# Linear attention, gated GLU and SoLU in one kernel: the first phase in nine equal blocks of 512 tokens

## The chip, the cores and the metric

The kernel runs on one core of one Trainium2 chip. The metric is the device time of one execution in microseconds; most executions of one kernel agree within 0.3%. The engines are TensorE (PE), VectorE (DVE), ScalarE (ACT), GpSimd (POOL) and SyncE (SP), which here only issues DMAs.

## The reference, cut to what matters

Inputs are double precision (the 64-bit weights are turned into pairs of single-precision parts on the chip, below). For 8 batches of 576 tokens, 8 heads of 64:

```python
q_s = exp(q - max(q, -1)); q_s /= sum(q_s, -1) + 1e-9        # softmax over the head dimension
k_s = exp(k - max(k, 2));  k_s /= sum(k_s, 2) + 1e-9         # softmax over the tokens of a batch
x = einsum('bhsd,bhde->bhse', q_s, einsum('bhsd,bhse->bhde', k_s, v))
x = x.transpose(0, 2, 1, 3).reshape(4608, 512)
g = x @ w_gate                                               # 512 x 1536
y = (g * sigmoid(g) * (x @ w_val)) @ w_out                   # 1536 x 512
h = y @ w_in                                                 # second layer, 512 x 1024
s = h * softmax(h)
out = ((s - mean(s)) / sqrt(var(s) + 1e-6) * g_ln) @ w_out2  # 4608 x 512
```

A block of tokens needs all k and v of its batch before its first product with x (the k softmax runs over the tokens), but only its own rows of q.

## The kernel before, in words

**Phase 1** makes y for all 4608 tokens and stores it; **phase 2** reads it back and does the second layer in 36 tiles of 128 tokens. Phase 2 is not touched except for where its tiles lie.

Products are made in single precision parts: every operand is a high part (rounded to the matmul's format) and a low part (the rest), and `mm3` does three matmuls for one product: high x high, high x low, low x high.

**Blocks and steps.** Phase 1 goes block by block over tokens. In a block, the 1536 inner columns are twelve steps `f` of 128. A step is 12 matmuls of the gate product (`emit_g`, then ScalarE's silu, L850), 12 of the output product of an earlier step (`next_o`, L805 to L807 into `y`), and 12 of the value product (`emit_v`, then `v_rest`: VectorE multiplies, `st`, L855; ScalarE rounds, `ah`, L859; VectorE subtracts, `al`, L861). The output product of step f comes two steps later. Gate and value products and all small products share four PSUM banks. The blocks before: two of 288 tokens (batch 0), seven of 512, one of 448.

**Weights.** Eighteen 1 MB pieces: twelve `wgv` (gate and value of one step) and six `wo` (output of two steps). Each comes as 64-bit words and is converted on the chip by `Weight.convert`, in five steps that a `Task` can take one by one: ScalarE scales the high words (L231), the low words are shifted down to three bits (L234 on ScalarE or L238 on VectorE, chosen by `l3`: before, two of three pieces on ScalarE), ScalarE writes the rounded high word over the upper half of the low word (L242), VectorE joins them (L245), rounds to the high part (L258) and subtracts for the low part (L260). Thirteen pieces fit in SBUF; eight `wgv` are stored after conversion and streamed in again for every later block through three slots (`STREAM`, `TURNS`). The pieces of the second layer's weights are converted one a block (`conv_w2`).

**The startup before.** A `Clock` puts the work of the startup in order by nominal times written in `KEYS`: tasks are taken by due time, one generator step at a time, and this fixes the order of each compute engine's instructions. The prologue makes batch 0's k-v products and x; the clock's stream `products` then runs the two 288-token blocks in two chunks of six steps (`fch`), block 0 and block 1 in turn, so that each converted weight serves both blocks before the next is wanted. Chunk one leaves a partial y of both blocks in DRAM (`y_part`), which `y_fix` adds in blocks 3 to 6. The conversions lie between the products by their times in `conv`; k, v and q of batch 1 and of the third block are loaded and worked off at the times `e0`, `e1`, `e2`, late in the startup.

**The blocks after the startup.** From the third block on, order is written out: `block` merges the steps (gate at position 3n, output at 3n+1, value at 3n+2) with a dictionary of extra tasks at such positions (`tasks_of`): k's maximum and exponential and k-v products of the next batch, q of the next block, its transposition by DMA (`q_turn`), its parts (`q_split`), its x (`x_mm`), weight streaming. Under `manual_schedule` each engine, SP included, runs its instructions in just this order.

Of the kernel before, what the change touches and what calls it, by code (L numbers as in the profile page):

```python
# [19 lines left out]
P = 128  # L20
# [7 lines left out]
    ld=(0, 1, 2, 5, 3, 6, 4, 8, 7),  # L28
# [10 lines left out]
    go=27.8,  # L39
    conv=(17.35, 22.1, 27.85, 28.0, 30.65, 34.25, 35.8, 40.3, 45.7, 50.5, 54.15, 58.15, 62.6, 68.25, 72.6, 77.45, 82.05, 87.15),  # L40
    q1=(23.5, 26.45, 29.5, 30.9, 32.2, 1.0),
    e0=(93.3, 94.1, 100.3, 102.55, 102.4),
    e1=(97.1, 107.55, 112.6, 116.3, 118.8),
    e2=(100.5, 110.4, 116.1, 120.3, 125.5, 1.5),
    warm=((3.5, 18), (10.25, 1), (15.02, 1), (18.81, 8), (19.15, 5), (19.65, 2), (22.83, 7), (25.42, 3), (29.44, 7), (30.61, 2), (34.75, 1)),
    store=(48.0, 50.0, 52.0, 54.0, 56.0, 90.0, 92.0, 94.0),
    banks=3,
    fch=(6,),
    l3=(3, 2),
    hi=(1, 0),  # L50
    d={'km': 1.3, 'kb': 0.5, 'rs': 1.3, 'kvh': 0.3, 'kvl': 0.3, 'qh': 0.4, 'ql': 0.4, 'xh': 0.4, 'xl': 0.5, 'w1': 1.1, 'w2': 1.0, 'w3': 1.0, 'w4': 1.3, 'w5': 1.1, 'mm': 0.37, 'ev': 1.0, 'ah': 0.6, 'al': 0.9, 'qn': 1.0},
    late=27.81,
# [65 lines left out]
def attention_glu_solu_kernel(  # L118
# [38 lines left out]
    QC = T // SP  # L157
# [34 lines left out]
    FCH = [range(a, b) for a, b in zip((0, *KEYS['fch']), (*KEYS['fch'], NF))]  # L192
# [4 lines left out]
    y_part = dram.tile([2, len(FCH) - 1, KD, P, T], F32, name="y_part")  # L197

# [5 lines left out]
    class Weight:  # L204
# [21 lines left out]
        def convert(self, pool, tag, bufs):  # L226
# [26 lines left out]
            if self.scales is None:  # L253
                hi, lo = (y.rearrange("p a m -> p (a m)") for y in (hi, lo))
                if (self.no or 0) % KEYS['hi'][0] < KEYS['hi'][1]:
                    nc.scalar.copy(out=hi, in_=x)
                else:
                    nc.vector.tensor_copy(out=hi, in_=x)  # L258
# [30 lines left out]
    def conv():  # L289

        n = len(conv_tasks)
        if n >= 2:
            conv_tasks[n - 2].finish()
        need(early_t or len([x for x in x_done if x[0] == 0]) == NPAIR)
        args = (att0, "t", 2) if early_t else (att, ("vt", "qt")[n % 2], 1)
# [22 lines left out]
    def weight(key):  # L318
        w, a = W[key]
        if w.no is not None:  # L320
            need(w.no < len(conv_tasks))
            conv_tasks[w.no].finish()
        return w.hi[:, a], w.lo[:, a]
# [7 lines left out]
    def stream_store(f):  # L331
        w, _ = W["wg", f]
        need(w.no < len(conv_tasks))
        conv_tasks[w.no].finish()
        w.store(w1_dram[streamed.index(f)])
# [30 lines left out]
    def stream_next(j, e):  # L366
# [5 lines left out]
        if STREAM[e] is None:  # L372
            load_w2(j - 2)
        else:
            stream_load(STREAM[e])
# [32 lines left out]
    def v_load(pool, b, h0):  # L408
        for t in conv_tasks:
            t.finish()  # L410
        need(b == 0 or len(conv_tasks) >= len(conv_todo))
# [156 lines left out]
    def q_load(pool, j, raw_pool=None, tag="qt"):  # L568
        b, half = divmod(j, 2)
        if j >= 2:  # L570
            x = pool.tile([BLOCKS[j][1] // 4, 4, H, D], F32, tag=tag, bufs=1, name=tag)
            for b, s, ps in segments(j):
                rows = q[b, :, s:s + 4 * (ps.stop - ps.start), :].rearrange(
                    "h (p c) d -> p c h d", c=4
                )
                for c in range(4):
                    nc.sync.dma_start(out=x[ps, c], in_=rows[:, c])
            qt_t[j] = x, x
            return
        qt_t[j] = heads_load(  # L580
            pool, tag, 1, q[b, :, half * T:(half + 1) * T, :], H, QC, raw_pool
        )
# [8 lines left out]
    def q_max(pool, j, hs):  # L591
        q_step(j, hs, 1)
        need(j != 1 or {(0, 0), (0, 1)} <= kv_done)
# [5 lines left out]
        nc.gpsimd.tensor_tensor(  # L599
# [8 lines left out]
    def q_norm(pool, j, hs):  # L608
# [7 lines left out]
        nc.gpsimd.tensor_tensor(  # L616
# [6 lines left out]
    def q_transpose(ps, pool, j, pr):  # L623
        qt = qt_t[j][1]
        need(q_at[j, 2 * pr] == 3 and len(qT_t) < 2)
        pq = ps.tile([P, QC, SP], F32, tag="gv", name="pq")
        for c in range(QC):
            nc.tensor.transpose(
                out=pq[:, c, :], in_=qt[:, c, 2 * pr:2 * pr + 2, :].rearrange("p h d -> p (h d)"), identity=ident[:SP, :SP]
            )  # L630
        qh = pool.tile([P, T], F32R, tag="qh", bufs=qb, name="qh")
        ql = pool.tile([P, T], F32R, tag="ql", bufs=qb, name="ql")
        qhv = qh.rearrange("e (p c) -> e c p", c=QC)
        qlv = ql.rearrange("e (p c) -> e c p", c=QC)
        yield d["qh"]
        nc.scalar.copy(out=qhv, in_=pq)
        yield d["ql"]
        nc.vector.tensor_tensor(out=qlv, in0=pq, in1=f32(qhv), op=ALU.subtract)
# [9 lines left out]
    def q_turn(pool, j):  # L648

        n = BLOCKS[j][1] // 4  # L650
        (wp, wt), tt = ((pool, "kt"), "vt") if j == 2 else ((tmp, "yt"), "qt")
        w = wp.tile([n, 2, 4 * H * D], U16, tag=wt, bufs=1, name="qw")
# [3 lines left out]
        qw_t[j] = wT = pool.tile([P, 2, 4, NPAIR, n], U16, tag=tt, bufs=1, name="qwT")  # L656
# [26 lines left out]
    def x_mm(ps, j, pr):  # L683
# [41 lines left out]
    def tasks_of(j):  # L725
# [7 lines left out]
        if j < B:  # L733
            for n, (load, rows, sub, exp, mm) in enumerate(((0, 2, 5, 9, 11), (12, 17, 20, 24, 26))):
                h0 = n * HG
                if n:
                    at(t, load, kv_load, att, j, h0)
                    at(t, load, v_load, att, j, h0)
                at(t, rows, kv_max_rows, att, j, h0)
                at(t, sub, kv_max_all, att, j, h0)  # L740
                at(t, exp, kv_exp, j, h0)
                for u in range(2):
                    at(t, mm, kv_mm, ps_at, att, j, h0, u)
        at(t, 15, conv_w2, j - 2, 3)
        at(t, 23, conv_w2, j - 2)
# [14 lines left out]
        at(t, 24, store_w2, j - 2)  # L760
        at(t, 25, stream_next, j, STREAM.index(None))
        if 3 <= j < 7:
            y_fix(t, (j - 3) // 2, 2 * ((j - 3) % 2))
        return t

    def kv_next(j):

        if j < B:
            kv_load(att, j, 0)
            v_load(att, j, 0)  # L770
# [8 lines left out]

    def y_fix(t, j, d):  # L780

        tiles = []

        def load(n, src):
            if not tiles:
                y = tmp.tile([P, 2, 2, T], F32, tag="yt", bufs=1, name="fix")
                tiles.extend((y[:, 0], y[:, 1]))
            nc.sync.dma_start(out=tiles[n], in_=src[d:d + 2].rearrange("k p t -> p k t"))

        def add():  # L790
            nc.vector.tensor_tensor(out=tiles[0], in0=tiles[0], in1=tiles[1], op=ALU.add)

        def store():
# [551 lines left out]
```

## Time and profile before

| | us |
|---|---|
| median of three runs | 1427.79 (1425.69 to 1430.31) |
| the profiled execution | 1428.78 |
| its span | 1426.9 |
| PE busy in the span | 1384.3 |
| DVE busy | 728.1 |
| ACT busy | 695.2 |
| POOL busy | 143.8 |
| first gate product starts | 36.30 |
| first gate product of the third block starts | 200.87 |

The span is the time between the first and the last instruction of the profiled execution. Busy times count an engine's own instructions. PE's is drawn out by overlapping matmuls, so a PE that is busy all the time may still be slower at a lower granted clock. A row of a view gives start, duration, engine, line of the kernel, operation, what it writes and reads, and in brackets how long the engine had been idle and what ended the wait.

### The profile page before, as it was taken

The page shows a single profiled execution, that of the slowest core. Times are in us where ns is not written, and L with a number is a line of the kernel's source. Part 1 is how long each engine was busy: PE and PEld are TensorE (multiplying, and loading weights), DVE is VectorE, ACT ScalarE, POOL GpSimd, SP SyncE. Part 2 cuts the span into 40 slices and gives each one's busy share as a digit, 9 for nine tenths or more (in the row PEclk, how much of TensorE's full clock was granted, in tenths as well). Part 3 has the DMA queues.
Part 4 walks back from the last instruction along what each step waited for, and adds up shares of the span by engine and source line. Part 5 has one row for each costly group of instructions (what it writes and reads, how often), then busy time and mean ns, then how long its engine had stood idle before and what let it go on. Part 6 is the DMA issues. An engine that isn't in the chain of part 4 may idle for free.

```text
span 1426.9 us, 18380 instructions
## 1 busy us (share of the span) xinstructions
PE 1384.3 (97%) x7263; PEld 1174.8 (82%) x7263; DVE 728.1 (51%) x1220; ACT 695.2 (49%) x927; POOL 143.8 (10%) x112
## 2 busy tenths in 40 slices
PE   7797899999999999999999999999999999999998
PEld 6797788888888888888888888899888888888887
DVE  6767744544544544434434422422257666666663
ACT  6986445425425425425525514331246665566563
POOL 3000302103103102102102002000000000000000
PEclk9899899999999999999999999999999999999999
DMA  9956285556566665675565263473334444544441
GB/s 257 344 168 183 62 208 171 122 164 189 136 170 171 149 181 146 152 194 139 143 179 143 99 193 92 148 265 118 144 73 104 104 97 78 106 97 101 103 78 37
DMA packets 255621, 207.11 MB, mean 145 GB/s; under 512 B 208048, under 2 KB 228528, under 8 KB 243760
## 3 DMA queue, kind: packets, MB, share of 16 engines
q1 hardware_dynamic: 255536, 205.95, 53.8%
q8 instruction: 57, 0.93, 0.3%
q14 instruction: 28, 0.23, 0.1%
HBM read 142.87 MB, written 38.01 MB: 127 GB/s over the span
## 4 chain that ended last, share of the span: by engine, by line
PE 85%; ACT 7%; DVE 5%; DMA 1%; issue 1%; POOL 0%; SPq 0%; ACTq 0%; DVEq 0%; POOLq 0%
PE wg L805 6%; PE y L806 6%; PE y L807 6%; PE y L805 6%; PE wv L805 6%; PE wv L807 6%; PE wv L806 6%; PE wg L807 6%; PE wg L806 6%; PE y L1236 4%; PE y L1235 4%; PE y L1234 4%; PE ph L1123 4%; PE ph L1125 4%; PE ph L1124 4%; PE pk L532 1%
## 5 line engine op out<-in xcount | busy, mean ns | idle before, releaser
L855 DVE TENSOR_TENSOR st<-st,wv 128x512 f32<-128x512 f32 (+2 forms) x120 | 75.9, 632 | 346.6 <-PE wv L807 320.4
L859 ACT CAST ah<-st 128x512 fp32r<-128x512 f32 (+2 forms) x120 | 70.5, 587 | 369.4 <-DVE st L855 369.3
L806 PE MATMUL y<-al,wo 128*128 128x512 f32 (+2 forms) x480 | 179.2, 373 | 8.5 <-DVE al L861 8.5
L805 PE MATMUL y<-ah,wo 128*128 128x512 f32 (+2 forms) x480 | 179.0, 373 | 8.7 <-ACT ah L859 5.3
L805 PE MATMUL wg<-xh,wgv 128*128 128x512 f32 (+2 forms) x480 | 180.2, 375 | 3.2 <-DVE wgv L258 3.2
L807 PE MATMUL wg<-xh,wgv 128*128 128x512 f32 (+2 forms) x480 | 178.2, 371 | 0.7 <-DVE wgv L260 0.7
L805 PE MATMUL wv<-xh,wgv 128*128 128x512 f32 (+2 forms) x480 | 178.5, 372 | 0.0
L807 PE MATMUL y<-ah,wo 128*128 128x512 f32 (+2 forms) x480 | 178.3, 372 | 0.0
L806 PE MATMUL wv<-xl,wgv 128*128 128x512 f32 (+2 forms) x480 | 178.1, 371 | 0.0
L807 PE MATMUL wv<-xh,wgv 128*128 128x512 f32 (+2 forms) x480 | 178.0, 371 | 0.0
L806 PE MATMUL wg<-xl,wgv 128*128 128x512 f32 (+2 forms) x480 | 178.0, 371 | 0.0
L861 DVE TENSOR_TENSOR al<-st,ah 128x512 fp32r<-128x512 f32 (+2 forms) x120 | 85.3, 711 | 68.5 <-ACT ah L859 68.4
L1236 PE MATMUL y<-w,zl 128*128 128x512 f32 (+1 forms) x296 | 113.7, 384 | 0.7 <-DVE zl L1205 0.7
L1234 PE MATMUL y<-w,zh 128*128 128x512 f32 (+1 forms) x296 | 113.6, 384 | 0.0
L1235 PE MATMUL y<-w,zh 128*128 128x512 f32 (+1 forms) x296 | 113.5, 383 | 0.0
L1123 PE MATMUL ph<-w,yh 128*128 128x512 f32 x288 | 112.9, 392 | 0.0
L1125 PE MATMUL ph<-w,yl 128*128 128x512 f32 x288 | 112.8, 392 | 0.0
L1124 PE MATMUL ph<-w,yh 128*128 128x512 f32 x288 | 112.6, 391 | 0.0
L806 PEld LDWEIGHTS y<-al,wo 128*128 128x128 f32 x480 | 91.9, 191 | 23.5 <-DVE al L861 9.8
L805 PEld LDWEIGHTS y<-ah,wo 128*128 128x128 f32 x480 | 91.6, 191 | 23.9 <-ACT ah L859 5.7
L850 ACT ACTIVATE st<-wg 128x512 f32<-128x512 f32 (+2 forms) x120 | 67.1, 559 | 88.7 <-PE wg L807 88.4
L805 PEld LDWEIGHTS wg<-xh,wgv 128*128 128x128 f32 x480 | 91.2, 190 | 17.4 <-DVE wgv L258 3.4
(239 smaller groups left out, 2424.2 us busy)
## 6 DMA issues: line engine op xcount, KB each, us to landing
wgv<-w_dram SPq DMA_DIRECT2D x64, 1024.0 KB, 5.3
vt<-in_v_dram SPq DMA_DIRECT2D x64, 144.0 KB, 4.7
yr<-y_dram SPq DMA_DIRECT2D x9, 1024.0 KB, 5.9
w_dram<-wgv SPq DMA_DIRECT2D x8, 1024.0 KB, 9.3
w_dram<-w2r SPq DMA_DIRECT2D x8, 1024.0 KB, 3.9
w<-w_dram SPq DMA_DIRECT2D x8, 1024.0 KB, 4.9
kt<-in_k_dram SPq DMA_DIRECT2D x56, 144.0 KB, 5.3
out_dram<-ot SPq DMA_DIRECT2D x58, 128.0 KB, 2.4
```

The costliest lines, as they stand in the source:

```text
L805: nc.tensor.matmul(out=po, lhsT=wh, rhs=rh, start=start, stop=False)
L806: nc.tensor.matmul(out=po, lhsT=wh, rhs=rl, start=False, stop=False)
L807: nc.tensor.matmul(out=po, lhsT=wl, rhs=rh, start=False, stop=stop)
L855: nc.vector.tensor_tensor(out=st, in0=st, in1=pv, op=ALU.mult)
L859: nc.scalar.copy(out=ah, in_=st)
L861: nc.vector.tensor_tensor(out=al, in0=st, in1=f32(ah), op=ALU.subtract)
L1123: nc.tensor.matmul(out=po, lhsT=yh[:, kk, s], rhs=wh, start=(kk == 0), stop=False)
L1124: nc.tensor.matmul(out=po, lhsT=yh[:, kk, s], rhs=wl, start=False, stop=False)
L1125: nc.tensor.matmul(out=po, lhsT=yl[:, kk, s], rhs=wh, start=False, stop=(kk == KD - 1))
L1234: nc.tensor.matmul(out=po[:, s], lhsT=zh[:, c, :], rhs=wh[:, s], start=first, stop=False)
L1235: nc.tensor.matmul(out=po[:, s], lhsT=zh[:, c, :], rhs=wl[:, s], start=False, stop=False)
L1236: nc.tensor.matmul(out=po[:, s], lhsT=zl[:, c, :], rhs=wh[:, s], start=False, stop=last)
```

## The change

Phase 1 goes in nine blocks of 512 tokens. The two 288-token blocks, their chunks, `y_part` and `y_fix` are gone. The prologue now loads 512 rows of q at once (128 partitions in place of 96) and transposes them on PE in four pieces a pair of heads; it ends with three converted weights and x of the first block. It runs to its end before the first product.

The first block then runs as the later ones do, by positions written out, with `first_tasks` in place of `tasks_of`. Fifteen conversions lie in its first ten steps, one in even steps and two in odd ones: the first three operations (L231, L234 or L238, L242) right behind the gate product of step n, the rest (L245, L258, L260) behind the value product of the same step, for weights that are used two steps later. `l3` now sends the shift of two of three pieces to VectorE. The temporary of the conversion has one buffer. Batch 1's k and v and the next q are loaded between the middle weights, worked off in the first block, and its large elementwise subtractions and products go to VectorE instead of GpSimd. k's maximum over a partition's six tokens is made by five elementwise maxima in every block. Later blocks keep their positions, with the batch worked off in block j now j + 1. Line numbers in the rows and in the text are those of the kernel before.

```diff
 KEYS = dict(
-    ld=(0, 1, 2, 5, 3, 6, 4, 8, 7),
+    ld=(0, 1, 2, 5, 3, 6, 4, 7),
...
-    conv=(17.35, 22.1, 27.85, 28.0, 30.65, 34.25, 35.8, 40.3, 45.7, 50.5, 54.15, 58.15, 62.6, 68.25, 72.6, 77.45, 82.05, 87.15),
...
+    conv=(17.35, 22.1, 27.85),
...
-    l3=(3, 2),
+    l3=(3, 1),
...
-    BLOCKS = [(0, T), (T, T)]
-    while BLOCKS[-1][0] + BLOCKS[-1][1] < NT:
-        c0 = sum(BLOCKS[-1])
-        BLOCKS.append((c0, min(TM, NT - c0)))
+    BLOCKS = [(c0, TM) for c0 in range(0, NT, TM)]
...
+    def conv_start(n):
+
+        need(n == len(conv_tasks) and not early_t)
+        conv_tasks.append(Task(conv_todo[n].convert, (tmp, "t2", 1)))
+        for _ in range(3):
+            conv_tasks[n].step()
+
+    def conv_end(n):
+
+        need(all(t.done for t in conv_tasks[:n]))
+        conv_tasks[n].finish()
...
-        nc.vector.tensor_reduce(
-            out=m, in_=raw.rearrange("p c h d -> p h d c"), axis=AX.X, op=ALU.max
-        )
+        for c in range(1, KC):
+            nc.vector.tensor_tensor(
+                out=m, in0=m if c > 1 else raw[:, 0], in1=raw[:, c], op=ALU.max
+            )
...
-    def q_max(pool, j, hs):
+    def q_max(pool, j, hs, eng=nc.gpsimd):
...
-        nc.gpsimd.tensor_tensor(
+        eng.tensor_tensor(
             out=qt, in0=raw, in1=qm.to_broadcast([n, nc_, nh, D]), op=ALU.subtract
         )
...
     man.enter_context(tc.manual_schedule())
-    for j in range(2, NB - 1):
+    for n, x in enumerate(mid):
+        if n == 3:
+            kv_next(0)
+        if n == 5:
+            q_next(0)
+        load_w1(w_b, f"b{n}", *x)
+    nc.sync.dma_start(out=g_sb, in_=g_ln.rearrange("(c p) -> p c", p=P))
+
+    def first_tasks():
...
+        t = {}
+        n_conv = len(conv_tasks)
+        again_tags = iter(("a0", "a1", "a3", "a4", "b0"))
+        for n in range(NF - 2):
+            for _ in range(1 + n % 2):
+                at(t, 3 * n, conv_start, n_conv)
+                at(t, 3 * n + 2, conv_end, n_conv)
+                nm, i = order[n_conv]
+                if nm == "wgv" and i in streamed:
+                    at(t, 3 * n + 3, stream_store, i)
+                n_conv += 1
+        need(n_conv == len(order))
+        for f in range(2):
+            at(t, 0, stream_store, f)
+        for n, x in enumerate(again):
+            tag = next(again_tags)
+            at(t, 3 * n + 2, load_w1, w_b if tag == "b0" else wpool, tag, *x)
+        at(t, 2, kv_max_rows, att, 1, 0)
+        at(t, 8, kv_max_all, att, 1, 0, HG)
+        at(t, 12, kv_exp, 1, 0)
+        at(t, 14, q_max, att, 1, ALLH, nc.vector)
+        at(t, 14, kv_mm, ps_at, att, 1, 0, 0)
+        at(t, 14, kv_mm, ps_at, att, 1, 0, 1)
+        at(t, 15, kv_load, att, 1, HG)
+        at(t, 15, v_load, att, 1, HG)
+        at(t, 18, q_exp, 1, ALLH)
+        at(t, 20, q_norm, att, 1, ALLH, nc.vector)
+        at(t, 24, q_turn, att, 1)
+        at(t, 26, kv_max_rows, att, 1, HG)
+        at(t, 26, kv_max_all, att, 1, HG, HG)
+        at(t, 29, x_tiles, ph1x, 1)
+        at(t, 30, kv_exp, 1, HG)
+        at(t, 32, kv_mm, ps_at, att, 1, HG, 0)
+        at(t, 32, kv_mm, ps_at, att, 1, HG, 1)
+        for p in range(NPAIR):
+            at(t, 29 + p, q_split, att, 1, p)
+            at(t, 31 + p, x_mm, ps_at, 1, p)
+        at(t, 33, kv_next, 1)
+        at(t, 34, q_next, 1)
...
+    block(0, range(NF), y_of(0), first_tasks())
+    for j in range(1, NB - 1):
         block(j, range(NF), y_of(j), tasks_of(j))
```

## Rows read from the trace of the kernel before

**Rows 1.** Busy time by stretch: length, busy by engine (instructions), granted clock, DMA share, GB/s
```profile
36.30:134.00 97.70, 83.33 (x568) 79.84 (x567) 70.92 (x99) 83.41 (x86) 3.34 (x2) 0.93 0.69 234
200.87:1026.00 825.13, 825.13 (x4235) 694.51 (x4234) 341.34 (x576) 326.56 (x440) 94.41 (x37) 1.00 0.56 159
```
**Rows 2.** The chain that ended last, in order of time: start, length, what
```profile
179.92 7.37 DMA qwT<-qw
```
**Rows 3.** Timeline: two steps of a 512-token block on VectorE; 448-token matmuls on PE
```profile
304.23 0.69 DVE L855 TENSOR_TENSOR st<-st,wv 128x512 f32<-128x512 f32 x1 [6.51 <-PE wv L807]
...
312.39 0.69 DVE L855 TENSOR_TENSOR st<-st,wv 128x512 f32<-128x512 f32 x1 [6.09 <-PE wv L807]
...
949.68 0.36 PE L806 MATMUL wv<-xl,wgv 128*128 128x448 f32 x1
...
951.30 0.37 PE L805 MATMUL wg<-xh,wgv 128*128 128x448 f32 x1
```
**Rows 4.** Timeline of VectorE at the end of the prologue
```profile
37.70 0.46 DVE L702 TENSOR_TENSOR xl<-y,xh 128x288 fp32r<-128x288 f32 x1
38.08 0.70 DVE L238 TENSOR_SCALAR wo0r<-wo0r 128x1024 uint32<-128x1024 uint32 x1
```
**Rows 5.** Timeline of ScalarE and VectorE in the startup: waits of one conversion
```profile
129.27 2.58 ACT L242 CAST wo5r<-wo5r 128x1024 f16<-128x1024 f32 x1 [2.62 <-DVE wo5r L238]
...
131.89 1.23 DVE L245 SCALAR_TENSOR_TENSOR t<-wo5r 128x1024 uint32<-128x1024 uint32 x1 [2.35 <-ACT wo5r L242]
```
**Rows 6.** Timeline: a conversion's pieces on ScalarE and VectorE
```profile
244.69 1.11 ACT L231 ACTIVATE w2r0r<-w2r0r 128x1024 f32<-128x1024 f32 x1
...
58.36 2.60 ACT L242 CAST wo1r<-wo1r 128x1024 f16<-128x1024 f32 x1
60.60 1.32 ACT L234 ACTIVATE wgv4r<-wgv4r,floor_bias 128x1024 uint32<-128x1024 uint8 x1
...
267.40 0.69 DVE L861 TENSOR_TENSOR al<-st,ah 128x512 fp32r<-128x512 f32 x1 [0.69 <-ACT ah L859]
268.01 1.22 DVE L245 SCALAR_TENSOR_TENSOR t<-w2r0r 128x1024 uint32<-128x1024 uint32 x1
269.26 0.69 DVE L258 CAST w2r<-t 128x1024 fp32r<-128x1024 f32 x1
269.99 1.23 DVE L260 TENSOR_TENSOR w2r<-t,w2r 128x1024 fp32r<-128x1024 f32 x1
```
**Rows 7.** VectorE by group from 200 us on; then timelines of k's and q's operations
```profile
L598 DVE TENSOR_REDUCE qm<-qt 128x32 f32<-128x2048 f32 x6 | 13.7, 2280 | 0.0
...
217.27 0.43 DVE L441 TRANSPOSE_TENSOR_REDUCE r<-m 96x8 f32<-96x256 f32 x1
...
219.39 0.44 DVE L457 STREAM_TRANSPOSE mt<-mb 96x256 f32<-96x256 f32 x1
...
233.58 0.15 DVE L542 TENSOR_SCALAR rs<-pk 128x1 f32<-128x1 f32 x1
...
235.30 0.16 DVE L542 TENSOR_SCALAR rs<-pk 128x1 f32<-128x1 f32 x1
...
145.61 1.28 ACT L523 ACT_TABLE_LOAD   x1
146.91 1.48 ACT L523 ACTIVATE kt<-kt 96x1536 f32<-96x1536 f32 x1
```
**Rows 8.** Timeline of VectorE: first split and last x part of a PE-bound block
```profile
279.61 0.46 DVE L666 COPY z<-qwT 128x512 uint16<-128x512 uint16 x1
...
297.04 0.68 DVE L702 TENSOR_TENSOR xl<-px,xh 128x512 fp32r<-128x512 f32 x1
```
**Rows 9.** Timeline of PE behind a gap in the startup
```profile
167.94 0.61 PE L806 MATMUL y<-al,wo 128*128 128x288 f32 x1 [2.53 <-DVE al L861]
...
172.66 0.44 PE L807 MATMUL wv<-xh,wgv 128*128 128x288 f32 x1
...
173.22 0.29 PE L807 MATMUL wv<-xh,wgv 128*128 128x288 f32 x1
```

More of the change, by code (lines that the diff above doesn't have):

```diff
@@ L254, in convert @@
                 hi, lo = (y.rearrange("p a m -> p (a m)") for y in (hi, lo))
[L255 to L258, printed above, removed]
+                nc.vector.tensor_copy(out=hi, in_=x)
                 yield d["w5"]
@@ L291, in conv @@
         n = len(conv_tasks)
[L292 to L295, printed above, removed]
+        args = (att0, "t", 2) if early_t else (tmp, "t2", 1)
+        if n >= args[2]:
+            conv_tasks[n - args[2]].finish()
         task = Task(conv_todo[n].convert, args)
@@ L566, in segments, with q_load @@
             done += m
[L568 to L578, printed above, removed]
-            return
-        qt_t[j] = heads_load(
-            pool, tag, 1, q[b, :, half * T:(half + 1) * T, :], H, QC, raw_pool
-        )
+    def q_load(pool, j, raw_pool=None):
+        n = BLOCKS[j][1] // 4
+        if raw_pool is not None:
+            raw = raw_pool.tile([n, H, 4, D], F32, tag="raw8", bufs=1, name="raw")
+            nc.sync.dma_start(
+                out=raw.rearrange("p h c d -> p h (c d)"),
+                in_=q[0, :, 0:4 * n, :].rearrange("h (p c) d -> p h (c d)", c=4),
+            )
+            qt_t[j] = raw.rearrange("p h c d -> p c h d"), lambda: pool.tile(
+                [n, 4, H, D], F32, tag="qt", bufs=1, name="qt"
+            )
+            return
+        x = pool.tile([n, 4, H, D], F32, tag="qt", bufs=1, name="qt")
+        for b, s, ps in segments(j):
+            rows = q[b, :, s:s + 4 * (ps.stop - ps.start), :].rearrange(
+                "h (p c) d -> p c h d", c=4
+            )
+            for c in range(4):
+                nc.sync.dma_start(out=x[ps, c], in_=rows[:, c])
+        qt_t[j] = x, x
     q_at = {}
@@ L778, in y_of @@
         return y_dram[:, :, BLOCKS[j][0]:sum(BLOCKS[j])]
[L780 to L793, printed above, removed]
-            nc.sync.dma_start(out=y_of(j)[d:d + 2].rearrange("k p t -> p k t"), in_=tiles[0])
-        need(len(FCH) == 2)
-        at(t, 6, load, 0, y_of(j))
-        at(t, 6, load, 1, y_part[j, 0])
-        at(t, 11, add)
-        at(t, 12, store)
     acts = {}
@@ L994, in attention_glu_solu_kernel @@
-    e = K["e2"]
-    clock.at(K["e0"][0], q_load, att, 2)
-    clock.at(e[0], q_max, att, 2, ALLH)
-    clock.at(e[1], q_exp, 2, ALLH)
-    clock.at(e[2], q_norm, att, 2, ALLH)
-    clock.at(e[3] - .01, x_tiles, ph1x, 2)
-    clock.at(e[3], q_turn, att, 2)
-    for p in range(NPAIR):
-        clock.at(e[4] + e[5] * p, q_split, att, 2, p)
-        clock.at(e[4] + e[5] * p + 2.0, lambda p=p: x_mm(ps_at, 2, p))
     for n, x in list(enumerate(early))[n_a:]:
         load_w1(wpool, f"a{n}", *x)
+    with tc.manual_schedule(engines=COMPUTE):
+        clock.run()
@@ L1008, in attention_glu_solu_kernel @@
+    early_t.clear()
+    pro.close()
+    pro_ps.close()
     wb = ExitStack()
     psA = ExitStack()
-    def late_loads():
-        for t in conv_tasks:
-            t.finish()
-        need(len(k_done) == NPAIR and not callable(qt_t[1][1]))
-        early_t.clear()
-        pro.close()
-        w_b = wb.enter_context(tc.tile_pool(name="wb", bufs=1, reuse_waits="tile"))
-        nc.sync.dma_start(out=g_sb, in_=g_ln.rearrange("(c p) -> p c", p=P))
-        for n, x in enumerate(mid):
-            load_w1(w_b, f"b{n}", *x)
-        w_bs.append(w_b)
@@ new lines, in attention_glu_solu_kernel @@
+    nc.sync.dma_start(out=g_sb, in_=g_ln.rearrange("(c p) -> p c", p=P))
[39 more added lines that the diff above has]
+        at(t, 34, q_next, 1)
+        for e, f in enumerate(STREAM):
+            if f is not None and e > STREAM.index(None):
+                at(t, 3 * f + 2, stream_next, 0, e)
+        return t
```

187 lines of the change are left out of this document (50 added, 137 removed).

## The prediction

> **What bounds the kernel now.** I read the busy times by stretch first. From the start of the third block (200.87 us) to the end of phase 1 (1026), TensorE is busy all the time at full granted clock, and VectorE and ScalarE are busy about 40% of it [rows 1]. So there only PE's own work counts. In the startup, from the first gate product at 36.30 us to 134, PE is busy 83.33 of 97.70 us at a granted clock of 0.93, ScalarE for as long, VectorE 70.92 us [rows 1]. The chain of waits says the same: up to 134 us it runs through the weight conversions, then through the second batch's k, v and q, as far as the transposing DMA of 7.37 us [rows 2]. All that the change can win or lose lies before the moment when the first block runs at PE's own pace. I call the start of the first gate product T0 (now 36.3) and the start of the first product of the block after the startup B (now 200.87).
>
> **What is fixed behind B.** One step of a 512-token block (gate, output, value product, 36 matmuls) takes 312.39 - 304.23 = 8.16 us, 0.2267 us a matmul; at 448 tokens it is (951.30 - 949.68) / 8 = 0.2025 us [rows 3]. Behind B the kernel now takes 1426.9 - 200.87 = 1226.0 us. After the change the blocks behind B are eight of 512 in place of seven of 512 and one of 448: 432 x 0.0242 = 10.5 us more. At B two output products are still owed; they grow from 288 columns (0.128 us a matmul, in proportion) to 512: 24 x 0.099 = 2.4 us. The last x products and one more batch border add about 0.6. So the new span is B + 1226.0 + 13.5 = B + 1239.5, and the change breaks even at B = 187.4. The two additions on VectorE for the partial y, and the DMAs around them, go; PE hides them today, so they are worth nothing. The output rows need fewer stores, at most 0.3 us at the very end.
>
> **If PE set the pace in the first block**, it would take 12 x 8.16 = 97.9, plus some 6 us, taken by columns, for the k-v products and the next x: 104 us. With T0 = 37.7 this is B = 142, a span of 1381. So the question is what the fifteen conversions do to the two engines that work beside PE.
>
> **T0.** The prologue keeps its order. Its last link is ScalarE's cast of weight 1, then VectorE, then the last x; the last x part starts at 37.70 [rows 4]. The second q block leaves VectorE, which saves one reduction, less than 2.3 us by its size; x, q and their products grow from 288 to 512 columns, 0.1 to 0.25 us an instruction on some eight instructions of the chain. The loads carry the same bytes up to here, with more q ahead of v. I take T0 = 37.7, with 36 to 41 as bounds.
>
> **The order that the change writes down.** Each engine runs its instructions in the order of the program; an instruction that waits holds all behind it. In the changed first block, step n issues on ScalarE: silu(n), then for each conversion of the step the 2^-112 scaling (L231) and the cast to the sign half (L242), then ah(n). On VectorE: the low-word shift (L238; for two of three conversions, none of these on ScalarE), st(n), al(n), and then the second half (L245, L258, L260) of each conversion of this step. Even steps have one conversion, with its shift on ScalarE; odd steps have two, both with the shift on VectorE. L242 needs the shift. The wait exists today: L242 of wo5 sits 2.62 us for VectorE's shift, and then VectorE sits 2.35 us for L242 [rows 5]. What is new is that both sit in each other's order in every pair step: the shift stands behind the former step's conversions, ah(n) stands behind both L242, al(n) behind ah(n), the second halves behind al(n).
>
> One cycle of a pair step and a single step, from X, when the shift lets L242 start. ScalarE: L242 occupies it 2.24 (58.36 to 60.60), L231 1.11, L242 2.24, so ah starts at X + 5.6. VectorE meanwhile has only a shift and st to do. al starts some 0.66 behind ah (behind st's 0.69 it waits 0.69 for ah, so st to al is 1.38), and the next instruction 0.61 behind al: X + 6.9. Second halves of 3.12 each (268.01, 269.26, 269.99, 1.23 less a start overlap): two of them end at X + 13.1. Then st(n+1), 1.38 to al, 0.61, one more second half 3.12, a shift of 0.70 [rows 3, 4, 6]: X + 18.9, where the next pair starts. ScalarE's own single conversion (some 4.6) lies inside. PE needs 16.3 for the two steps and waits. So each cycle costs 18.9 plus whatever else stands on VectorE between a single's second half and the next shift, and the change puts just there:
> - step 2: the k maximum across rows, 2.56 (217.27 to 219.83), and its subtraction, now on VectorE, 96x1536: 1.8 (between 1.7 and three times the 0.69 of 512 columns): 4.4.
> - step 4: q's maximum 2.28 and its subtraction, same size, 2.3 (at most four times 0.69, 2.8); then two k-v tails of 1.72 each, VectorE and ScalarE by turns: 8.0. Behind them ScalarE reloads the silu table, does silu and L231 before it can start L242: 1.6 more. 9.6.
> - step 6: q's sum, reciprocal and product 5.1, and the exponential with its table load on ScalarE, which delays ah by 0.6: 5.7.
> - step 8: the q copy 1.1, k's maximum in five instructions of 96x256 at 0.44, 2.2 (today one reduction), maximum across rows and subtraction 4.4: 7.7.
> Together 27.4 [rows 3, 7]. On the way these operations were hidden today where they run in PE-bound blocks; here their cover is gone.
>
> Start: the conversion of wo0 now ends behind the last x. L242 for it starts at T0 + 2.6, its second half ends at 8.4, then st(0), ah(0) behind conversion 2's first half at 11.2, al, second half to 15.6, k's maximum 2.2, shift: X of the first pair = T0 + 18.5. The first weight of step 2 is there at about T0 + 15.6, while PE would want it at 10.9.
>
> End: the last pair's second halves end at X + 13.1. Behind them stand the four q splits and x casts, which take 297.04 + 0.68 - 279.61 = 18.1 us in a PE-bound block [rows 8], here with an exponential (1.48 and a table load, 1.28) and two k-v tails (3.4) in the same order; less some overlap, 23.5.
>
> Sum: B = 37.7 + 18.5 + 4 x 18.9 + 27.4 + 13.1 + 23.5 = 195.8. Span 195.8 + 1239.5 = 1435.3. The profiled execution took 1428.78 for a span of 1426.9, so 1.9 more: 1437.2. It lies 1.0 above the median of the runs shown (1427.79), so I predict 1436, 0.6% slower.
>
> The table loads: here a load is 1.28 us and the next instruction starts 0.02 behind it [rows 7]. The Trainium skill (ScalarE: Activation LUTs, "What ACT_TABLE_LOAD costs") counts a drain of about 1.38 us on top, 2.66 a switch. That is not what this trace shows; by the page the three switches on the path would add some 4 us, an estimate that I leave out.
>
> **Loads and queues.** SP now issues k and v of batch 1 behind three of the seven middle weights and the next q behind five, and must pass each in order. The seven weights are 7.3 MB, k, v and q 2.2 MB; at the 234 GB/s of this stretch [rows 1] all 9.6 MB are there 41 us after T0, while the last of the weights is wanted at about 75. The k of batch 1 is wanted 15.6 behind T0 and has four loads' time, some 16 us: it may cost a few us, or nothing. I take nothing. The stores of converted weights and the reloads into their slots wait in SP's queue for PE and VectorE, but each has two or more steps until it is used. POOL has only two fills in this block and nothing queues behind them.
>
> **Rivals.**
> 1. Full overlap (other side). The order costs nothing, because waits are short and each engine catches up; then the busiest engine's sum ends the block. VectorE's is 12 x 1.38 + 16 x 3.12 + 10 x 0.7 + about 35 for k, q and x = 108.5; B = 146, time 1387. For it: each of the three sums is within 108. Against: rows 5, both directions. Decides if pair steps start 8 to 9 us apart. 0.08.
> 2. Half overlap: the extra VectorE work falls into its 5 us of idle time per pair, so the 27.4 mostly vanish; about 1411. It would need an order other than the one written. 0.12.
> 3. Near even, 1424 to 1432: as forecast, with cycles 1 to 2 us shorter or a shorter end. 0.17.
> 4. Slower still: PE's clock. After a gap of 2.53 us at 167.94, matmuls of 288 columns last 0.44 us in place of 0.29 until 172.9, the lower of the two levels, 1.2 in place of 2.4 GHz [rows 9]. At half rate for 5 us, each such gap costs PE 2.5 us, as much as its slack of 18.9 - 16.3 in a cycle without extra work. If PE then ends the steps, the ten gaps of the block add up to some 12 us on top: 1448. 0.15.
> The rule of the Trainium skill for rival 4 (TensorE: Matmul & The Clock Gate, "What's actually happening") is that "the default state is throttled, and activity releases the throttle"; these rows agree.
>
> **Chances.** Forecast 0.48, its own range 1427 to 1447 (T0 -1.7 to +3, cycles +-1 each, the end +-4). With the rivals: 0.2 faster by over 0.3% (below 1423.5; 0.3% is about what can be told from no change), 0.17 within, 0.63 slower. For eight in ten I take 1412 to 1451.
>
> **What would show it.** Right: in the first block, VectorE's L245 waits for ah or L242 in each odd step, L242 waits for L238, pair steps lie 23 to 28 us apart, wgv products wait for L258 or L260, granted clock below 0.95, B near 196, behind it no idle PE. Wrong: B under 187; pair steps 16 to 17 us apart; long waits for DMA in the block; PE idle behind B.

## The result and the profile after

The changed kernel takes 1439.58 us, the median of four runs (1438.16 to 1440.36), where the kernel before took 1427.65 in the same series (1425.69 to 1430.31). The ratio is 1.0081, with a 95% interval of 1.0063 to 1.0100: slower by 0.8%. 1436.0 was predicted, with 1412 to 1451. The profiled execution of after took 1439.01 us for a span of 1436.8. One execution of ten in experiment 3 took 2610.55 us where the other nine took 1424 to 1426; all times are medians. Line numbers from here on are those of the changed kernel.

Busy time by stretch of after, the answer to [rows 1]; columns: length, busy of PE, PEld, DVE, ACT and POOL (instructions), granted clock, DMA share, GB/s.

```profile
46.00:198.70 152.70, 111.47 (x511) 88.53 (x511) 103.03 (x145) 95.67 (x88) 0.28 (x2) 0.82 0.60 167
198.70:1028.00 829.30, 829.30 (x4197) 688.76 (x4196) 329.90 (x618) 328.84 (x439) 94.37 (x37) 1.00 0.54 153
```

The first block ends at B = 198.64 (before, the point that answers to it is 200.87, but by then 576 tokens are done there, here 512). In the block no engine is busy all the time: PE 73%, VectorE 67%, ScalarE 63% of 152.70 us. The block lasts 1.37 times as long as the busiest engine works in it; when all have slack, a chain that runs from one to the other sets the time. The waits of the same stretch say between which two (engine, waiting operation, what it waits for: us in all, times, the longest):

```profile
DVE al L819 <- ACT ah L818: 33.9, 11, 7.0
...
PE px L684 <- ACT qh L663: 16.3, 1, 16.3
ACT kvh L535 <- DVE rs L531: 12.1, 4, 8.8
...
PE pk L520 <- ACT kt L511: 10.2, 1, 10.2
ACT wgv11r L226 <- DVE wgv11r L222: 9.5, 1, 9.5
...
ACT wgv5r L226 <- DVE wgv5r L222: 7.3, 1, 7.3
ACT wgv9r L226 <- DVE wgv9r L222: 6.7, 1, 6.7
```

VectorE waits for ScalarE's ah, ScalarE's cast (L226, before L242) waits for VectorE's shift (L222, before L238), by turns: both directions of [rows 5], now in each other's order. After the st at 47.48 us and until 196, neither of the two waits once for PE, and in the whole stretch none of the three waits for a DMA. So PE follows: the first gate product of step 2 starts 0.15 us behind the cast of its weight (L239, before L258).

```profile
54.21 0.69 DVE L239 CAST wgv<-t 128x1024 fp32r<-128x1024 f32 x1
...
55.05 0.47 PE L771 MATMUL wg<-xh,wgv 128*128 128x512 f32 x1 [2.23 <-DVE wgv L239]
```

The gate products at 68.28, 121.27 and 146.35 start 0.15 us behind their cast too, though the view puts these waits down to a shift on ScalarE that had ended long before. ScalarE's timeline at the casts that open the five pair steps:

```profile
59.01 2.58 ACT L226 CAST wgv3r<-wgv3r 128x1024 f16<-128x1024 f32 x1 [5.17 <-DVE wgv3r L222]
82.70 2.60 ACT L226 CAST wgv5r<-wgv5r 128x1024 f16<-128x1024 f32 x1 [7.27 <-DVE wgv5r L222]
112.01 2.58 ACT L226 CAST wgv7r<-wgv7r 128x1024 f16<-128x1024 f32 x1
137.21 2.60 ACT L226 CAST wgv9r<-wgv9r 128x1024 f16<-128x1024 f32 x1 [6.72 <-DVE wgv9r L222]
164.19 2.55 ACT L226 CAST wgv11r<-wgv11r 128x1024 f16<-128x1024 f32 x1 [9.52 <-DVE wgv11r L222]
```

The starts lie 23.69, 29.31, 25.20 and 26.98 us apart; PE would need 16.3. In the first cycle ScalarE's ah stands behind the second cast of the pair:

```profile
62.53 2.58 ACT L226 CAST wo1r<-wo1r 128x1024 f16<-128x1024 f32 x1
64.78 0.76 ACT L818 CAST ah<-st 128x512 fp32r<-128x512 f32 x1
```

The same cycle on VectorE, from the wait for ah to the next shift:

```profile
65.57 0.69 DVE L819 TENSOR_TENSOR al<-st,ah 128x512 fp32r<-128x512 f32 x1 [5.45 <-ACT ah L818]
66.18 1.22 DVE L229 SCALAR_TENSOR_TENSOR t<-wgv3r 128x1024 uint32<-128x1024 uint32 x1
...
72.55 0.68 DVE L815 TENSOR_TENSOR st<-st,wv 128x512 f32<-128x512 f32 x1
73.92 0.69 DVE L819 TENSOR_TENSOR al<-st,ah 128x512 fp32r<-128x512 f32 x1 [0.69 <-ACT ah L818]
...
77.65 0.43 DVE L429 TRANSPOSE_TENSOR_REDUCE r<-m 96x8 f32<-96x256 f32 x1
...
81.93 0.68 DVE L222 TENSOR_SCALAR wgv5r<-wgv5r 128x1024 uint32<-128x1024 uint32 x1
```

The shift that ScalarE wants from 75.43 on stands behind a second half and k's maximum, until 81.93.

### The profile page after: what moved, and what is told of

It is laid out like the page before. It is cut to its first block, busy times and chain, and to the rows that moved or that the text cites. A ratio compares the mean times of both kernels' runs of the same rounds, so it can differ in the third digit from the quotient of the medians.

```text
span 1436.8 us, 17350 instructions
## 1 busy us (share of the span) xinstructions
PE 1376.1 (96%) x6813; PEld 1134.8 (79%) x6813; DVE 709.5 (49%) x1240; ACT 685.0 (48%) x884; POOL 125.3 (9%) x106
## 4 chain that ended last, share of the span: by engine, by line
PE 85%; DVE 5%; ACT 4%; issue 2%; DMA 2%; POOL 0%; SPq 0%; DVEq 0%; ACTq 0%
PE wg L771 6%; PE y L771 6%; PE y L773 6%; PE y L772 6%; PE wv L771 6%; PE wv L772 6%; PE wv L773 6%; PE wg L772 6%; PE wg L773 6%; PE y L1175 4%; PE y L1174 4%; PE y L1173 4%; PE ph L1063 4%; PE ph L1064 4%; PE ph L1062 4%
## 5 line engine op out<-in xcount | busy, mean ns | idle before, releaser
L815 DVE TENSOR_TENSOR st<-st,wv 128x512 f32<-128x512 f32 x108 | 74.1, 687 | 363.0 <-PE wv L773 335.6
L771 PE MATMUL wg<-xh,wgv 128*128 128x512 f32 x432 | 174.6, 404 | 15.0 <-ACT wgv10r L218 5.6
L773 PE MATMUL wg<-xh,wgv 128*128 128x512 f32 x432 | 172.6, 399 | 0.8 <-DVE wgv L241 0.8
L772 PE MATMUL wg<-xl,wgv 128*128 128x512 f32 x432 | 172.1, 398 | 1.1 <-DVE xl L691 1.1
L771 PE MATMUL wv<-xh,wgv 128*128 128x512 f32 x432 | 169.4, 392 | 0.0
L773 PE MATMUL wv<-xh,wgv 128*128 128x512 f32 x432 | 169.1, 391 | 0.0
L772 PE MATMUL wv<-xl,wgv 128*128 128x512 f32 x432 | 169.1, 391 | 0.0
L771 PE MATMUL y<-ah,wo 128*128 128x512 f32 x432 | 168.5, 390 | 0.0
L773 PE MATMUL y<-ah,wo 128*128 128x512 f32 x432 | 168.2, 389 | 0.0
L772 PE MATMUL y<-al,wo 128*128 128x512 f32 x432 | 168.1, 389 | 0.0
L819 DVE TENSOR_TENSOR al<-st,ah 128x512 fp32r<-128x512 f32 x108 | 74.7, 692 | 99.1 <-ACT ah L818 99.1
L771 PEld LDWEIGHTS wg<-xh,wgv 128*128 128x128 f32 x432 | 83.3, 193 | 34.7 <-ACT wgv10r L218 6.0
L773 PEld LDWEIGHTS wg<-xh,wgv 128*128 128x128 f32 x432 | 83.2, 193 | 20.9 <-DVE wgv L241 3.2
L772 PEld LDWEIGHTS wg<-xl,wgv 128*128 128x128 f32 x432 | 83.4, 193 | 18.5 <-DVE xl L691 2.0
```

Source lines behind the costliest of these rows:

```text
L771: nc.tensor.matmul(out=po, lhsT=wh, rhs=rh, start=start, stop=False)
L772: nc.tensor.matmul(out=po, lhsT=wh, rhs=rl, start=False, stop=False)
L773: nc.tensor.matmul(out=po, lhsT=wl, rhs=rh, start=False, stop=stop)
L815: nc.vector.tensor_tensor(out=st, in0=st, in1=pv, op=ALU.mult)
L819: nc.vector.tensor_tensor(out=al, in0=st, in1=f32(ah), op=ALU.subtract)
```

## The experiments

The theory: the order written down couples ScalarE and VectorE, and PE waits for the weight that comes out of it. The rivals: the amount of work on one engine, and PE's lower clock. B is the start of the first gate product of the second block, read from each trace; "cycles" are the four distances between casts, as above. The kernel before ran in every series and took 1427.65 to 1428.04 us in each.

What lies behind B is not quite fixed. In the profiled executions it is 1236.8 us in 1, 7 and 9, 1239.6 in 6 and 10, and 1238.1 to 1238.5 in the others. In the 12 us from B + 844 on, where phase 2 starts, the granted clock is 1.00 in the first group, 0.72 in the second and 0.86 in the third. So up to 2.9 us of the difference between two such executions need not come from the first block, and for small differences B is given too.

**1. The shifts to ScalarE.**

```diff
-            if (self.no or 0) % KEYS['l3'][0] < KEYS['l3'][1]:
+            if (self.no or 0) > 2 or (self.no or 0) % KEYS['l3'][0] < KEYS['l3'][1]:
```

> All shifts of the first block's conversions on ScalarE: ten of them (1.33 us each) move there from VectorE (0.69 us each). Theory (the order: the cast waits for the shift, which stands behind the former step's second halves): the waits of 9.5, 7.3, 6.7 and 5.2 us of the cast for the shift go. A cycle of a pair and a single step is then 18.5 us (ah of the pair, al and two second halves 6.9, st 0.7, ah of the single 0.6, silu 0.5, two full conversions on ScalarE 9.3) plus what is left of VectorE's extra work over some 5 us of slack (0, 4.6, 0.3, 2.7): 82 us for four cycles in place of 105.2, so about 23 us faster than the changed kernel, 1413 to 1420. Rival (the amount of work on ScalarE, the engine with the longest sum beside PE, sets the block): 13 us more of it, so 1440 to 1452. Rival (PE's lower clock sets the block): no difference, 1438 to 1441.

Measured: 1420.89 us (1420.02 to 1422.30), 18.7 less than after; ratio to before 0.9953 (0.9938 to 0.9968). B is 183.73, the cycles 18.72, 31.55, 20.61 and 19.85. More work on ScalarE made the block faster, so ScalarE's sum is not the bound. The time lies 0.9 us above the range expected: one cycle stayed at 31.55, in which kvh waits 8.80 us for VectorE.

**2. The shifts earlier, nothing else.** A conversion now takes the shift ahead of the scaling, and a pair's shifts stand one step earlier. The lines of the edit that place them (`conv_shift` does only the shift):

```diff
+                if n % 2:
+                    at(t, 3 * n - 2, conv_shift, n_conv)
                 at(t, 3 * n, conv_start, n_conv)
```

> The shifts of a pair step's two conversions stay on VectorE, but are issued one step earlier, behind the former pair's second halves and ahead of the single step's st; no instruction is added. Theory (order): the cast of a pair no longer waits for a single step's second half and the extra work behind it; cycle about 16.3 plus the part of the extra work over 2.6 us of slack (1.3, 7, 2.7, 5.1), 81 us for four in place of 105.2: 1412 to 1420. Rival (amount of work on either engine, or PE's clock): no engine has less to do, so 1437 to 1442.

Measured: 1418.85 us (1418.23 to 1419.93), 20.7 less than after with the same instructions; ratio to before 0.9942 (0.9924 to 0.9959). B is 179.37, the cycles 17.65, 31.61, 19.02, 19.50: order, not amount. The long cycle is again the one of step 4; ScalarE and VectorE there:

```profile
96.92 0.63 ACT L551 ACTIVATE kvh<-pk,rs 64x64 fp32r<-64x64 f32 x2 [8.80 <-DVE rs L547]
98.65 0.63 ACT L551 ACTIVATE kvh<-pk,rs 64x64 fp32r<-64x64 f32 x2 [1.10 <-DVE rs L547]
99.30 1.28 ACT L826 ACT_TABLE_LOAD   x1
100.59 0.60 ACT L826 ACTIVATE st<-wg 128x512 f32<-128x512 f32 x1
```

```profile
91.89 2.28 DVE L606 TENSOR_REDUCE qm<-qt 128x32 f32<-128x2048 f32 x1
94.27 2.29 DVE L607 TENSOR_TENSOR qt<-qt,qm 128x2048 f32<-128x2048 f32 x1
96.48 0.15 DVE L546 TENSOR_SCALAR rs<-pk 128x1 f32<-128x1 f32 x1
...
108.89 0.69 DVE L835 TENSOR_TENSOR al<-st,ah 128x512 fp32r<-128x512 f32 x1 [6.97 <-ACT ah L834]
```

kvh waits for two operations on q that it does not need, silu and two conversions queue behind kvh, and VectorE then waits for their ah.

**3 and 5. The second halves one gate product later.**

```diff
-                at(t, 3 * n + 2, conv_end, n_conv)
+                at(t, 3 * n + 4, conv_end, n_conv)
...
-                    at(t, 3 * n + 3, stream_store, i)
+                    at(t, 3 * n + 5, stream_store, i)
```

> The second halves of a step's conversions move behind the next step's gate product, ahead of that step's st, and the store of the converted weight with them; all instructions and their durations stay. Theory (order): the shift then stands behind al alone, ah behind casts that wait for nothing, and the second halves fill the time in which VectorE waited for ah. PE's 98 us and some 6 us for k-v products and x, plus at most 15 us of VectorE's extra work over its slack: the first product of the second block starts at 150 to 168 us in place of 198.64, 1388 to 1408 us. Rival (amount of work): 1437 to 1442. Rival (loads and stores: 23 MB in this block at the 290 GB/s of its busiest stretch is 80 us): it would end no sooner than 44 + 80 and so not be seen here.

Measured: 1424.57 us (nine of ten executions 1423.98 to 1425.69), ratio to before 0.9982 (0.9972 to 0.9991). 15.0 less than after, but 17 to 37 more than expected. The kernel ran again for its profile (1424.35).

> The same kernel as with the second halves behind the next gate product, for a profile of it (its time is 1424.6, where 1388 to 1408 was expected). It tells which expectation failed. Theory (order, elsewhere): VectorE still sits for ScalarE in every second step, because silu of a step now waits for a gate product whose weight is finished later, or the cast waits for a shift behind it; then long waits of al for ah or of the cast for the shift stay, and VectorE is busy below 75% between 46 and 185 us. Rival (VectorE's amount of work): VectorE is busy above 90% and waits for nothing long. 1423 to 1427.

VectorE is busy 103.75 of 139.00 us (75%), B is 184.13. The casts still wait 2.06, 3.33, 3.63 and 5.94 us for shifts, and what is new is that PE waits 6.74, 2.06, 6.18 and 4.68 us for second halves. VectorE around the first of these:

```profile
53.53 1.79 DVE L417 TENSOR_TENSOR m<-m,kt 96x256 f32<-96x256 f32 x4
55.24 0.68 DVE L222 TENSOR_SCALAR wgv3r<-wgv3r 128x1024 uint32<-128x1024 uint32 x1
55.84 0.68 DVE L222 TENSOR_SCALAR wo1r<-wo1r 128x1024 uint32<-128x1024 uint32 x1
56.45 1.22 DVE L229 SCALAR_TENSOR_TENSOR t<-wgv2r 128x1024 uint32<-128x1024 uint32 x1
57.70 0.69 DVE L239 CAST wgv<-t 128x1024 fp32r<-128x1024 f32 x1
```

The second half that the next gate product needs now stands behind k's maximum and two shifts. My expectation had counted what no longer waits, and not the shorter time left for the moved work. It was the order again, elsewhere.

**4 and 12. The large elementwise operations to GpSimd.** In the first block `q_max` and `q_norm` lose `nc.vector` and `kv_max_all` loses its last argument.

> The four large elementwise operations of the first block (k's two subtractions, q's subtraction and product; 1.75, 2.29, 2.29 and 1.75 us on VectorE) go to GpSimd, where the kernel before had them at 3.4 to 3.6 us each. Theory: steps 2, 4, 6 and 8 lose 8.1 us on VectorE's chain, less what VectorE's two-operand instructions lose beside GpSimd (some 2 us a piece where they overlap) and what the later readers wait: 1430 to 1438, 2 to 8 us faster than the changed kernel. Rival (these operations were hidden, or PE's clock sets the block): 1438 to 1446.

Measured: 1430.54 us (1429.89 to 1433.04), 9.0 less than after. The cycles are 21.88, 26.93, 22.83 and 25.77, shorter by 1.8, 2.4, 2.4 and 1.2. So the extra VectorE work did count almost in full: 8.1 us taken off it made the four cycles 7.8 shorter in sum, although one shift beside GpSimd's 3.88 us lasted 4.11 in place of 0.69. What gave the rest of the 9.0 was not tried. It repeated:

> The changed kernel with its four large elementwise operations on GpSimd a second time, on another chip if one is given, because 9 us of gain stand against a loss of 2 us for the same edit in the better order: the gain is real if it is 8 to 10 us again (1429.5 to 1431.5), and an accident of that series if it is under 5 us (above 1434.5).

Measured: 1430.63 us (1429.98 to 1431.69).

**6. The k-v products ahead of q, on top of 2.**

```diff
-        at(t, 14, q_max, att, 1, ALLH, nc.vector)
         at(t, 14, kv_mm, ps_at, att, 1, 0, 0)
         at(t, 14, kv_mm, ps_at, att, 1, 0, 1)
+        at(t, 14, q_max, att, 1, ALLH, nc.vector)
```

> As with the early shift (1418.85), and in step 4 the two k-v products stand ahead of q's maximum and subtraction (one swap of neighbours at one position). There the profile of the early shift shows ScalarE's kvh 8.80 us behind the rows' sum on VectorE, which is queued behind 4.6 us of q's maximum and subtraction; silu and two conversions are queued behind kvh, and al then waits 6.97 us. Theory (order): 4 to 5 us faster, 1413 to 1416. Rival (VectorE's amount of work sets the block): not over 1 us faster, 1417.5 to 1420.

Measured: 1412.59 us (1412.27 to 1416.69), 6.3 less than 2, where 4 to 5 were expected. kvh waits 4.21 in place of 8.80, al 3.64 in place of 6.97, the second cycle is 27.00 in place of 31.61. B is 174.99, 4.4 earlier than in 2; the profiled execution is the longest of the four (1416.69).

**7. GpSimd on top of 6.**

> As the run with the k-v products ahead, and the four large elementwise operations of the first block on GpSimd, which by itself made the changed kernel 9 us faster (1430.54 against 1439.58). Theory (VectorE has become the engine without idle time, so that 8.1 us less on it count nearly in full): 1404 to 1408. Rival (now PE's own pace or ScalarE bounds the block, or two-operand instructions on VectorE lose as much beside GpSimd): 1411 to 1417.

Measured: 1414.65 us (1413.83 to 1415.40), 2.1 more than 6: the theory's number failed. VectorE beside GpSimd:

```profile
78.60 2.31 DVE L835 TENSOR_TENSOR al<-st,ah 128x512 fp32r<-128x512 f32 x1 [1.27 <-ACT ah L834]
...
106.01 0.69 DVE L835 TENSOR_TENSOR al<-st,ah 128x512 fp32r<-128x512 f32 x1 [5.43 <-ACT ah L834]
...
125.07 1.43 DVE L835 TENSOR_TENSOR al<-st,ah 128x512 fp32r<-128x512 f32 x1 [2.35 <-ACT ah L834]
...
146.33 2.84 DVE L835 TENSOR_TENSOR al<-st,ah 128x512 fp32r<-128x512 f32 x1 [0.69 <-ACT ah L834]
```

Three al took 4.5 us more than 0.69 each, and the waits for ah grew (5.43 for 3.64, 2.35 for 0.69): the cycles are within 0.5 us of those of 6, and B is 175.94. So 4.5 of the 8.1 us came back as longer al, and some as waits for ScalarE; no run separates the two. The same edit was worth 9 us in one order and nothing in another.

**8. The join ahead of al, on top of 6.** The step that follows the cast to ah now issues L229 first (numbered L238 here).

```diff
         nc.scalar.copy(out=ah, in_=st)
+        if j == 0 and i in join:
+            conv_tasks[join[i]].step()
         nc.vector.tensor_tensor(out=al, in0=st, in1=f32(ah), op=ALU.subtract)
```

> As the run with the k-v products ahead (1412.59), and in the first block's steps 0 to 9 the join of the first conversion stands between st and al on VectorE in place of behind al, where VectorE otherwise sits 0.69 us for ScalarE's ah. Theory (between 54 and 154 us VectorE has no other idle time left and is the chain): 0.6 us in each of the steps with that wait, some eight of them, so 4 to 6 us faster, 1406.5 to 1409. Rival (PE or ScalarE ends the steps there): within 1 us, 1411.5 to 1413.5.

Measured: 1407.71 us (1406.86 to 1408.29), 4.9 less than 6; B is 167.96. The 0.69 us of idle time is filled:

```profile
68.45 1.22 DVE L238 SCALAR_TENSOR_TENSOR t<-wgv4r 128x1024 uint32<-128x1024 uint32 x1
69.59 0.69 DVE L837 TENSOR_TENSOR al<-st,ah 128x512 fp32r<-128x512 f32 x1
```

**9. The first q split earlier, on top of 8.**

```diff
-            at(t, 29 + p, q_split, att, 1, p)
+            at(t, 29 + p if p else 28, q_split, att, 1, p)
```

> As the join ahead of al, and the first q split of the next block stands ahead of step 9's st, in place of behind its two second halves, where PE sat 9.06 us for its qh. Theory (the end is one more place of the same kind: PE's x product is queued ahead of the value product of step 10 and waits for VectorE's list): 4 to 8 us faster than the join alone. Rival (the second halves of the last weights, now 2 us later, take its place): 0 to 2 us faster.

Measured: 1403.28 us (1402.53 to 1404.20), 4.4 less than 8; PE's wait ahead of the first x product fell from 9.80 to 2.30 us. B is 165.39, only 2.6 earlier than in 8, and 1.6 us of the difference between the two profiled executions lie behind it; so in these two the block gained less than the 4 to 8 us expected. This is the fastest version: 0.9825 of before (0.9810 to 0.9840) and 36.3 us below after.

**10. A shift of each pair to ScalarE, on top of 9.** The condition of the shift gets `or late and self.no % 3 == 2`, where `late` means a conversion of the first block.

> As the run before in this list, and the shift of each pair's wo goes to ScalarE, at its early place, where ScalarE waits for st (3.6, 1.0, 0.9, 0.4, 0.5, 3.1 us). Theory (VectorE is the chain, ScalarE has slack there): 0.6 us for each of four or five pairs, 1 to 3 us faster. Rival (ScalarE is as near to the end of a step as VectorE): the 1.3 us of each shift show, 1 to 5 us slower.

Measured: 1407.36 us (1406.59 to 1408.18), 4.1 more than 9. ScalarE is the busier of the two now (46 to 169 us: 101.65 against 99.39), and VectorE waits for ah 1.65, 1.18, 1.77 and 1.98 us where in 9 it waits 0.98, not at all, 2.40 and 0.30. But B is 166.56, only 1.2 later than in 9, and the other 2.8 us between the two profiled executions lie behind B, where both kernels run the same instructions. So the edit did not pay, and a loss of 4 us in the block is not shown.

**11. k's exponential earlier, on top of 9.**

```diff
-        at(t, 12, kv_exp, 1, 0)
+        at(t, 11, kv_exp, 1, 0)
```

> As the run with the join ahead of al and the first q split ahead of step 9's st (1403.28), and k's exponential of the first heads stands ahead of silu and conversion of step 4 on ScalarE in place of behind them; PE sat 3.8 us for it ahead of the k-v products. Theory (PE, with 104.5 of 119 us busy, is now near to being the bound, so a wait of PE is worth most of itself): 2 to 4 us faster. Rival (VectorE's list still ends step 5, and the exponential now delays ah of step 4): within 1 us, or up to 3 us slower.

Measured: 1404.37 us (1403.83 to 1404.79), 1.1 more than 9; the intervals of the two ratios to before overlap (0.9819 to 0.9848 here). The total agrees with the rival. Busy time of 9, then of 11, in the first block (columns as in the first fence):

```profile
46.00:165.00 119.00, 104.51 (x507) 83.74 (x506) 100.42 (x143) 96.62 (x88) 0.28 (x2) 0.93 0.78 219
```

```profile
46.00:165.00 119.00, 103.12 (x516) 81.41 (x515) 101.10 (x144) 95.67 (x89) 0.38 (x2) 0.97 0.80 221
```

PE's wait went and its granted clock rose from 0.93 to 0.97. B is 163.63, 1.8 earlier than in 9, and 1.6 us more lie behind B. So the block did get shorter in the profiled execution, by a little less than the theory's 2 to 4, and the total hides it. Whether the wait or the clock gave it was not tried.

## Why the prediction was right

**Behind B.** 1239.5 was forecast; it is 1436.8 - 198.64 = 1238.2, and 1236.8 to 1239.6 in the ten other kernels. Of 36 us between the slowest and the fastest version 33 lie ahead of B, as the prediction said; the spread of 2.9 behind B goes with the granted clock at the start of phase 2 (above), which the prediction did not count.

**The order.** The forecast's mechanism, L242 behind the shift, ah behind both L242, al and the second halves behind ah, is what the two timelines show, and experiment 2 shows it alone: the same instructions, the shifts one step earlier, 20.7 us, 19.3 of them ahead of B. Two of the signs came out otherwise: the wait on VectorE stands on al, just ahead of the second half that was named, and one distance (29.31) lies above the 23 to 28. In that cycle the cast waits for nothing, because ScalarE itself is late: kvh had waited 8.80 us.

**The terms.** In the cycle shown, from X = 59.01 the second halves end at X + 13.54 (forecast 13.1), the single step's part takes 5.10 (5.11), the extra work 4.28 (4.4), shift to cast 0.77 (0.70). A cycle without extra work is 19.41 in place of 18.9, four of them 2.0 us more. If the others are reckoned with 19.41 too, their extra work is 9.90, 5.79 and 7.57, with 4.28 together 27.5 (27.4): cover that is gone costs the whole duration. Against the forecast itself the cycles are 0.4, 0.8, 0.6 and 0.4 us longer.

**T0 and the start** were off, against each other, and that they partly cancel is luck. The prediction calls T0 the first gate product, but reckons with the last x part, 37.70 [rows 4], so I compare that one (the first gate product now starts at 32.57, between the x parts). The last x part of the prologue:

```profile
41.99 0.69 DVE L691 TENSOR_TENSOR xl<-y,xh 128x512 fp32r<-128x512 f32 x1
```

That is 4.3 later, 1.0 past the bound of 41 that I gave. The first pair then starts 17.02 behind it, not 18.5: ScalarE comes to ah(0) at 9.6, not 11.2, and the rest is as forecast. What delays the prologue was not tried. VectorE's first maximum over q waits 2.28 us for the load of q, which I had priced at nothing. The cast of the second weight starts at 34.20, before at 30.31, so 3.9 of the 4.3 us arise ahead of it; from what stays open.

**The end.** From X of the last pair to B it takes 34.45, not 36.6, and not by the path forecast. The second halves end at X + 13.45 (13.1), but the 21.0 behind them (23.5) are not VectorE's splits and casts: PE starts its first x product at 178.84 and is not idle again but for 0.3 us.

```profile
178.84 0.42 PE L684 MATMUL px<-qh,kvh 128*128 128x64 f32 x1 [16.25 <-ACT qh L663]
...
181.28 0.63 PE L771 MATMUL wv<-xh,wgv 128*128 128x512 f32 x1
181.71 0.63 PE L772 MATMUL wv<-xl,wgv 128*128 128x512 f32 x1
...
198.64 0.39 PE L771 MATMUL wg<-xh,wgv 128*128 128x512 f32 x1
```

Behind a gap of 16.25 us it runs at the lower of its two levels (granted clock 0.50) until 185.12, with 0.43 us from one 512-column matmul to the next in place of 0.23. At the full clock the 15 matmuls of that stretch would take some 3 us less, an estimate from these distances. So this term came near the forecast by another mechanism than the one in it, which is luck too.

Together: +4.3 - 1.5 + 2.0 + 0.1 - 2.1 = +2.8, which is 198.64 against 195.8. Behind B it is 1.3 us less, and from the span to the median 2.8 in place of 0.7: 1439.58 against 1436.

**The rivals.** Full overlap (B = 146) didn't come by itself, and the best reorderings reach 163.63 to 165.39; half overlap needs another order, as said, and 6 to 9 are such orders. PE's clock: the granted clock of the block is 0.82, and 0.70 from 164 to 198.70. In the cycles it costs nothing, since VectorE and ScalarE, which set them, never wait there for PE; at the end it costs some 3 us, as said. So this rival holds for the end alone, and not to the 12 us that it named. The table load shows 1.28 us and the next instruction 0.01 behind it (99.30, then 100.59 in experiment 2), as in [rows 7], so the drain of the Trainium skill's page (ScalarE: Activation LUTs, "What ACT_TABLE_LOAD costs") was rightly left out.

**Experiments 3, 7 and 10** missed where they took work or waits off one engine and assumed that the other had time. The prediction itself had followed both engines' orders through a cycle, and came out within 0.8 us a cycle.

## What to carry to other kernels

When two in-order engines hand pieces to each other within a step, write down both orders and follow one cycle through them; busy shares of 63 to 73% on every engine, with waits of two of them for each other and for nothing else, were the sign of such a loop here, and no engine's sum predicted it. Put the instruction that the other engine waits for ahead of work that nobody waits for (the shift one step earlier 20.7 us, the k-v products ahead of q 6.3 us, an instruction in the wait for ah 4.9 us), and only then balance the amounts. What an engine's spare work costs depends on the order: the same four operations were worth 9 us in one and nothing in the other. When an edit is worth a few microseconds, compare the stretch that it changes and not the totals: here the rest of the kernel moved by up to 2.9 us.

## What the runs showed of the hardware that was not expected

Where a VectorE instruction was delayed beside one of GpSimd, it was not slowed down by a share but held to its end. The GpSimd operations of experiment 7 beside which the three al lie:

```profile
76.83 3.53 POOL L466 TENSOR_TENSOR kt<-kt,mt 96x1536 f32<-96x1536 f32 x1 [52.85 <-DMA wgv9r<-in_moe_w_gate_dram]
...
122.33 3.63 POOL L624 TENSOR_TENSOR qt<-qt,qs 128x2048 f32<-128x2048 f32 x1 [19.17 <-DVE qs L622]
...
145.15 3.47 POOL L466 TENSOR_TENSOR kt<-kt,mt 96x1536 f32<-96x1536 f32 x1 [19.20 <-DVE mt L461]
```

They end at 80.36, 125.96 and 148.62, the three al at 80.91, 126.50 and 149.17: 0.54 to 0.55 us later each time, whenever al began; the shift of 4.11 us in experiment 4 ends 0.55 behind GpSimd's product. The Trainium skill (SBUF — State Buffer, "SBUF: two separate sides") says that the two share a port pair under an exclusive lock, held for the whole instruction by the one that starts first; these rows agree. Two pairs of shifts in experiment 4 were not held; the first shift of each began just before GpSimd's operation. One of them:

```profile
79.37 0.65 DVE L222 TENSOR_SCALAR wgv5r<-wgv5r 128x1024 uint32<-128x1024 uint32 x1
79.52 4.49 POOL L450 TENSOR_TENSOR kt<-kt,mt 96x1536 f32<-96x1536 f32 x1 [55.95 <-DMA wgv9r<-in_moe_w_val_dram]
79.94 0.68 DVE L222 TENSOR_SCALAR wo2r<-wo2r 128x1024 uint32<-128x1024 uint32 x1
```

There GpSimd's operation was the longer one, 4.49 us here and 4.42 at 155.06, in place of 3.53 and 3.47 in experiment 7. The held shift followed another that had also begun before GpSimd, so who waits is not settled by that alone, and no run here shows what does.
